# Attention with forget gates and an MLP on one core: the opening order rewritten, the first keys and queries in two token parts, w_in in column quarters

## The chip, the cores and the metric

The program runs on one core of a Trainium2 chip. The metric is device time in microseconds of one execution, the median over several. Three runs of the kernel before gave 329.88, 330.83 and 330.89 us, so the median is 330.83 us. One further execution was recorded by the hardware profiler; every row below is from that one.

## The reference

```python
def _attn_ref(q, k, v, f):            # each 8 batches, 8 heads, 576 tokens, 64 wide; f without the 64
    scores = scale * np.matmul(q, k.transpose(0, 1, 3, 2))
    cum = np.cumsum(np.log(np.clip(f, 0.0001, 1.0)), axis=-1)
    decay = cum[:, :, :, None] - cum[:, :, None, :]
    scores = np.where(causal, -1000000000.0, scores + decay)
    scores = scores - np.max(scores, axis=-1, keepdims=True)
    attn = np.exp(scores)
    attn = attn / (np.sum(attn, axis=-1, keepdims=True) + 1e-09)
    return np.matmul(attn, v)
...
x = attn_out.transpose(0, 2, 1, 3).reshape(4608, 512)
h = x @ w_in                          # 512 x 2048
g = 0.5 * h * (1.0 + np.tanh(c * (h + 0.044715 * h * h * h)))
return g @ w_out                      # 2048 x 512
```

All inputs and the output are float32; the kernel multiplies in bfloat16.

## The kernel before

**Tiling.** The 64 pairs of batch and head are worked in 16 *quads* of four heads (quad i is batch i // 2, heads 4 (i % 2) to 4 (i % 2) + 3). The 4608 tokens are worked through the MLP in nine *chunks* of 512. A chunk can start when the attention of its tokens is done, so chunk 0 needs the quads 0 and 1 (batch 0), chunk 1 the quads 2 and 3 as well, and so on.

**One quad.** Keys and queries (288 KB each as bfloat16) are loaded by POOL with a cast (`load_one`, L185), one load for all 576 tokens. VectorE turns each into its transposed form (`transpose_words`, L191). TensorE multiplies keys by queries (`scores`, L238) in rounds; ScalarE takes the exponential (L264); the diagonal blocks are masked by POOL (L270, word M) or by a VectorE product (L299, word m). TensorE forms denominators (word D) and the attention output (word V); VectorE scales the latter into `xT` (L355). The values are multiplied by the decay weights into `vw` (L210; word VW on POOL, vw on VectorE). The quads 0 and 1 are split by tokens into a part of 256 and a part of 320 (`parts`, L183; `split_rounds`, L60), so that the MLP of the first 256 tokens (*half tile*, `mlp_in_half`, L450) can start early.

**The MLP.** Chunk 0's first product runs in eight half-tile pieces (word J.half.g: 16 matmuls of 256 columns, then one Gelu of 128x1024 on ScalarE). Piece g needs the columns 512 g to 512 g + 511 of w_in. Its second product (`mlp_out`, L565) is a generator that is pulled in units of one 128-token tile by one block of 128 rows of w_out: the words F.0.n and f.0.n pull n units; f uses four matmuls of 32 columns for each of F's one of 128. There are 64 units, tile by tile, 16 blocks each. Chunk 1's first product is the word I (eight times, L369), its second is `seven_products` (L491), pulled by F.1.n and f.1.n. From chunk 2 on a table for each chunk (`TABLES`) says the order; these tables do the same work before and after the change.

**Order.** Nothing is scheduled by the machine: every engine runs its own instructions in the order in which the program emits them. `setup` (L584) emits the first loads, fills and the transposes of log f; then `FRONT` (L73), a string of words, says the order up to the start of chunk 2. `@` after a word makes its first DMA wait for a named earlier one. Words: LK, LQ load keys and queries, TK, TQ transpose them; WI loads a quarter of w_in (a column half of two of the four row blocks, L173), WO a quarter of w_out (four of its 16 row blocks); LP, LX load values on POOL's queue, LU, LV on SP's; S and H emit scores for four or for two heads; CW makes the decay weights; U sums blocks of w_out; X and Y load ScalarE's table for Exp and for Gelu; CL copies the low block of `vw`; B.n.c emits n matmuls of c columns on zeros, which only keep TensorE busy.

**Queues.** Loads that cast can only be issued by POOL. POOL issues them in its own instruction order, between masks and `vw`. At most eight POOL loads are in flight: the ninth waits for the first of them. All loads share 16 DMA engines.

**Pools.** `psS` has two buffers for scores and half-tile pieces, `psO` one for D and V, `psM` two for the split D and V and for the second product.

Of the kernel before, what the change touches and what calls it, by code (L numbers as in the profile page):

```python
# [8 lines left out]
FP32 = mybir.dt.float32  # L9
# [7 lines left out]
def kernel(  # L17
# [28 lines left out]
    CH = 512  # L46
# [22 lines left out]
    SETUP = """  # L69
        TK.0 LP.4 LP.0 LP.1  # L70
    """

    FRONT = """  # L73
        TQ.0 B.2.256 TK.1 SB TR LP.2@LQ.0 B.2.128 CW S.0.0 B.5.384 B.1.256 Z TQ.1 vw.0.0 S.0.2 WI.0 LQ.2 M.0.0 B.3.384 H.1.0.1
        LP.3 B.1.256 vw.1.0 WI.1@LU.4 W H.1.1.1 WI.3 B.2.256 WI.2 H.1.0.0 M.1.0.1 D.0.0 M.1.0.0 H.0.1.1 V.0.0.0 H.0.1.0 B.2.256 M.0.1 H.1.1.0 V.0.1.0
        D.1.0 H.0.3.0 B.2.128 V.1.0.0 LX.1.1 H.0.3.1 V.1.1.0 m.0.3.2 H.1.3.0 m.0.3.4 B.1.256 VW.1.1 H.1.3.1 B.4.128 vw.0.1 D.0.1 M.1.3 S.1.2 M.1.1 LK.2
        V.0.1.1 V.0.0.1 WO.0 J.0.1 D.1.1 J.0.0 WO.1@LV.1.1 V.1.1.1 V.1.0.1 J.0.3 WO.2@WI.1 VW.3 J.1.0 WO.3 LK.3 LQ.3 J.1.1 TQ.2 J.1.3 LQ.4
        LX.1.0@WO.2 TK.2 J.0.2 J.1.2 X LK.4 F.0.6 TK.3 B.3.256 S.2.0 LK.5 F.0.9 S.2.2 F.0.10 S.2.1 TQ.3 TQ.4 F.0.10 LV.2.0@LK.5 m.2.1 vw.2
        TK.4 S.3.0 f.0.1 M.2.2 CL.2 LQ.5 M.2.0 D.2 f.0.6 S.3.1 m.3.0 F.0.6 V.2.0 S.3.2 TK.5 LK.6 M.3.2 f.0.7 V.2.1 CL.3
        S.4.1 m.3.1 LQ.6 F.0.6 TQ.5 H.4.2.1 D.3 H.4.0.1 LQ.7 VW.4 H.4.0.0 V.3.1 v.3.0 f.0.3 H.4.2.0 CL.4 I.1.0 m.4.1 U.0 LV.2.1@LQ.5 I.1.4  # L80
        TQ.6 m.4.2.3 I.1.1 I.1.5 U.1 LV.3.0@LQ.7 m.4.2.2 TK.6 G.0 M.4.0 I.1.2 I.1.3 U.3 I.1.6 I.1.7 G.1.1.2 U.2 X F.1.14 S.5.0 f.1.28 S.5.1 D.4 M.5.0 f.1.16
        S.5.2 V.4.0 m.5.2.3 f.1.10 VW.5 V.4.1 CL.5 m.5.2.2 LQ.8 S.6.0 f.1.10 M.5.1 D.5 f.1.7 S.6.1 V.5.1 f.1.12 V.5.0 vw.6 S.6.2
        m.6.1 M.6.2.2 m.6.0 m.6.2.3 LK.7 LK.8 CL.6 LX.3.1@LK.6
# [4 lines left out]
    TABLES.update(dict.fromkeys((2, 5), """  # L88
        Y O.512 P.0 P.1 TK.q3 TQ.q3 LK.q5 LQ.q5 TK.q4 TQ.q4 LK.q6 LQ.q6 LV P.4 P.5 G.0 P.2 P.3 P.6 P.7 G.1.1.2 X F.10 S.q3.0
        D.q2 M.q3.0 f.22 S.q3.1 V.q2.0 M.q3.1 VW.q3 f.18 S.q3.2 V.q2.1 M.q3.2 CL.q3 f.16 S.q4.0 D.q3 M.q4.0 f.18 S.q4.1 V.q3.0  # L90
        M.q4.1 VW.q4 f.9 V.q3.1 f.7 S.q4.2 M.q4.2 CL.q4
    """))
    TABLES.update(dict.fromkeys((3,), """
        Y O.512 P.0 P.1 TK.q3 TQ.q3 LK.q5 LQ.q5 TK.q4 TQ.q4 LK.q6 LQ.q6 LV K.1.0 K.1.1 K.1.2 P.4 P.5 G.0 P.2 P.3 P.6 P.7 G.1.1.2
        X F.10 S.q3.0 D.q2 M.q3.0 f.22 S.q3.1 V.q2.0 M.q3.1 VW.q3 f.18 S.q3.2 V.q2.1 M.q3.2 CL.q3 f.16 S.q4.0 D.q3 M.q4.0 f.18
        S.q4.1 V.q3.0 M.q4.1 VW.q4 f.9 V.q3.1 f.7 S.q4.2 M.q4.2 CL.q4
    """))
    TABLES.update(dict.fromkeys((4,), """
        Y O.512 P.0 P.1 TK.q3 TQ.q3 LK.q5 LQ.q5 TK.q4 TQ.q4 LK.q6 LQ.q6 LV K.3.0 K.3.1 K.3.2 P.4 P.5 G.0 P.2 P.3 P.6 P.7 G.1.1.2
        X F.10 S.q3.0 D.q2 M.q3.0 f.22 S.q3.1 V.q2.0 M.q3.1 VW.q3 f.18 S.q3.2 V.q2.1 M.q3.2 CL.q3 f.16 S.q4.0 D.q3 M.q4.0 f.18  # L100
        S.q4.1 V.q3.0 M.q4.1 VW.q4 f.9 V.q3.1 f.7 S.q4.2 M.q4.2 CL.q4
    """))
    TABLES.update(dict.fromkeys((6,), """
        Y O.512 P.0 P.1 TK.q3 TQ.q3 LK.q5 LQ.q5 LV P.4 P.5 G.0 P.2 P.3 P.6 P.7 G.1.1.2 X F.10 S.q3.0 D.q2 M.q3.0 f.22 S.q3.1
        V.q2.0 M.q3.1 VW.q3 f.18 S.q3.2 V.q2.1 M.q3.2 CL.q3 f.16 D.q3 f.18 V.q3.0 v.q3.1 T K.1.3 K.3.3 f.18
    """))
    TABLES.update(dict.fromkeys((7,), """
        Y O.512 P.0.1 R.1 P.4.1 R.1 R.1 R.3 P.2.1 R.3 G.0.1.2 P.6 R.3 G.0.3.4 G.1.1.2 T
    """))
    TABLES.update(dict.fromkeys((8,), """  # L110
        O.512 P.0.1 R.1 P.4.1 R.1 R.1 R.3 P.2.1 R.3 G.0.1.2 P.6 R.3 G.0.3.4 G.1.1.2
    """))
# [60 lines left out]
    def load_w_in(c):  # L173
        n, u = D_FF // 2, c % 2
        s = slice(n * (c // 2), n * (c // 2 + 1))
        return nc.gpsimd.dma_start(out=w_in_sb[:, 2 * u:2 * u + 2, s], in_=w_in_hbm[:, u, :, s])
# [8 lines left out]
    def load_one(src, dst, i):  # L185
        b, h0 = i // QPB, 4 * (i % QPB)
        return nc.gpsimd.dma_start(
            out=dst[i % 2].rearrange("p a d -> p (a d)"),
            in_=src[b, h0:h0 + 4].rearrange("h (p a) d -> (h p) (a d)", p=32))

    def transpose_words(src, dst):  # L191

        nc.vector.transpose(  # L193
            out=dst.rearrange("p s c -> p (s c)").bitcast(FP32)
                .rearrange("p (t a) -> p a t", a=S // 32),
            in_=src.rearrange("p a d -> p (a d)").bitcast(FP32)
                .rearrange("p (a d) -> p a d", d=D // 2),
        )

    def transpose_k(i):  # L200
        transpose_words(k_c[i % 2], kT[i % 2][:, 64:64 + S])

    def transpose_q(i):
        transpose_words(q_c[i % 2], qT[i % 2])
# [245 lines left out]
    def mlp_in_half(half, g):  # L450

        ph = psS.tile([128, 2, 512], FP32, name="ps_h", tag="s")
        n0 = QA * half
        for dts in (range(N_DT - 1), range(N_DT - 1, N_DT)):
            for j in range(4):
                ft = 4 * g + j
                for dt in dts:
                    nc.tensor.matmul(  # L458
                        ph[:, j // 2, QA * (j % 2):QA * (j % 2) + QA],
                        w_in_sb[:, dt, 128 * ft:128 * ft + 128],  # L460
                        xT[:, dt, n0:n0 + QA],
                        start=(dt == 0 and j % 2 == 0), stop=(dt == N_DT - 1),
                        skip_group_check=True,
                    )
        nc.scalar.activation(gT[:, 4 * g:4 * g + 4, n0:n0 + QA],
                             ph.rearrange("p a (b n) -> p (a b) n", n=QA), AF.Gelu_apprx_tanh)
# [98 lines left out]
    def mlp_out(c):  # L565

        for n in range(CH // 128):
            r0 = CH * c + 128 * n
            st = ostage_pool.tile([128, D_MODEL], FP32, name="o_st", tag="o")
            pso = psM.tile([128, D_MODEL], FP32, name="pso", tag="m")  # L570
            for ft in range(N_FT):
                cols = 32 if by_columns else 128
                for c0 in range(0, 128, cols):
                    nc.tensor.matmul(pso[c0:c0 + cols, :],  # L574
                                     gT[:, ft, 128 * n + c0:128 * n + c0 + cols],
                                     w_out_sb[:, ft, :],
                                     start=(ft == 0), stop=(ft == N_FT - 1), skip_group_check=True)
                if ft == N_FT - 1:
                    nc.vector.tensor_copy(st, pso)
                    nc.sync.dma_start(out=out[r0:r0 + 128, :], in_=st)  # L580
                yield


    def setup():  # L584
# [195 lines left out]
```

## Time and profile before

| what | value |
|---|---|
| span of the profiled execution, first to last instruction | 328.4 us |
| median of the three timed runs | 330.83 us, 2.4 us above that span |
| TensorE busy | 316.9 us (96%) |
| ScalarE, VectorE, POOL busy | 201.7, 206.4, 110.6 us |
| moved by DMA | 33.42 MB, 16.58 MB of it on POOL's queue |
| chain that ended last, TensorE's share | 86% |
| first score matmuls of quad 0, start | 9.78 us |
| first exponential of quad 0, start | 10.64 us |
| first half-tile piece (J.0.1), start | 24.94 us |
| first scores of quad 3 (S.3.0), start | 51.17 us |
| start of chunk 1's first product, of chunk 2's | 66.93 us, 102.42 us |

The profile gives busy time by engine, the span cut into 40 slices, groups by source line, and the chain of work that ended last, followed back from the last instruction to what released each step. A stretch can be cut out and its busy time and DMA rate read alone. Matmuls are pipelined: a row's busy time is a little longer than what it adds to the chain.

### The profile page before, as it was taken

The page shows a single profiled execution, that of the slowest core. Times are in us where ns is not written, and L with a number is a line of the kernel's source. Part 1 is how long each engine was busy: PE and PEld are TensorE (multiplying, and loading weights), DVE is VectorE, ACT ScalarE, POOL GpSimd, SP SyncE. Part 2 cuts the span into 40 slices and gives each one's busy share as a digit, 9 for nine tenths or more (in the row PEclk, how much of TensorE's full clock was granted, in tenths as well). Part 3 has the DMA queues.
Part 4 walks back from the last instruction along what each step waited for, and adds up shares of the span by engine and source line. Part 5 has one row for each costly group of instructions (what it writes and reads, how often), then busy time and mean ns, then how long its engine had stood idle before and what let it go on. Part 6 is the DMA issues. An engine that isn't in the chain of part 4 may idle for free.

```text
span 328.4 us, 11961 instructions
## 1 busy us (share of the span) xinstructions
PE 316.9 (96%) x5421; PEld 206.5 (63%) x5421; DVE 206.4 (63%) x323; ACT 201.7 (61%) x231; POOL 110.6 (34%) x155
## 2 busy tenths in 40 slices
PE   3999999999999999999999999999999999999995
PEld 1458844545776477646774577557754777787684
DVE  4686039884887865674567456636553767875772
ACT  4685576866767586668656775768675841721630
POOL 8985572510504415520544054303440140000000
PEclk9999999999999999999999999999999999999999
DMA  7999999861124990295129711761110102002012
GB/s 123 210 214 215 168 230 199 167 165 24 36 40 94 236 208 31 94 187 108 37 68 182 140 37 36 160 122 36 36 66 0 36 21 81 2 32 98 0 35 96
DMA packets 44323, 33.42 MB, mean 102 GB/s; under 512 B 27488, under 2 KB 37856, under 8 KB 44272
## 3 DMA queue, kind: packets, MB, share of 16 engines
q0 software_dynamic: 8848, 16.58, 28.0%
q1 hardware_dynamic: 35280, 16.01, 18.4%
q8 instruction: 42, 0.69, 0.9%
q14 instruction: 9, 0.07, 0.1%
q10 hardware_dynamic: 144, 0.07, 0.1%
HBM read 36.85 MB, written 9.44 MB: 141 GB/s over the span
## 4 chain that ended last, share of the span: by engine, by line
PE 86%; DMA 3%; DVE 3%; ACT 3%; POOL 2%; issue 2%; POOLq 0%; DVEq 0%; ACTq 0%
PE ps_h L369 29%; PE ps_w L504 25%; PE po L324 9%; PE ps_s L256 8%; PE pso L574 4%; PE ps_h L458 4%; DMA v_nat<-in_v_dram 2%; PE ps_cd L417 2%; ACT pt L264 2%; PE ps_ab L417 2%; PE po_m L310 1%; POOL vw L210 1%; DMA out_dram<-o_st 1%; POOL v_nat L164 0%; PE ps_o L324 0%
## 5 line engine op out<-in xcount | busy, mean ns | idle before, releaser
L264 ACT ACTIVATE pt<-ps_s 128x1024 bf16<-128x1024 f32 (+2 forms) x100 | 93.7, 988 | 39.4 <-PE ps_s L256 34.9
L369 PE MATMUL ps_h<-xT,w_in_sb 128*128 128x512 bf16 x448 | 99.0, 379 | 0.0
L376 ACT ACTIVATE gT<-ps_h 128x1024 bf16<-128x1024 f32 x56 | 57.2, 1022 | 49.9 <-PE ps_h L369 48.3
L270 POOL TENSOR_SCALAR_AFFINE_SELECT pt<-pt 128x512 bf16<-128x512 bf16 (+3 forms) x65 | 38.2, 597 | 132.9 <-ACT pt L264 131.8
L369 PEld LDWEIGHTS <-w_in_sb 128*128 128x128 bf16 x448 | 43.8, 98 | 50.1 <-issue 0.4
L504 PEld LDWEIGHTS <-gT 128*32 128x32 bf16 (+1 forms) x1253 | 50.9, 97 | 6.4 <-issue 1.7
L504 PE MATMUL ps_w<-w_out_sb,gT 128*32 128x256 bf16 (+1 forms) x1056 | 46.9, 273 | 0.0
L504 PEld LDWEIGHTS <-gsum 128*32 128x32 bf16 (+1 forms) x1256 | 38.9, 97 | 2.7 <-issue 1.4
L256 PE MATMUL ps_s<-qT,kT 32*128 32x64 bf16 (+5 forms) x896 | 36.8, 263 | 0.3 <-ACT pt L264 0.2
L483 DVE TENSOR_TENSOR gsum<-gT 128x1024 bf16<-128x1024 bf16 x16 | 11.0, 689 | 35.2 <-ACT gT L376 35.2
L504 PE MATMUL ps_w<-usum,gsum 128*32 128x256 bf16 (+1 forms) x832 | 30.7, 273 | 1.0 <-ACT snap L525 0.7
L355 DVE TENSOR_TENSOR xT<-po,rb 128x576 bf16<-128x576 f32 x26 | 19.6, 755 | 18.9 <-PE po L324 18.6
L193 DVE STREAM_TRANSPOSE kT<-k_c 128x576 f32<-128x576 f32 x16 | 20.0, 1247 | 17.8 <-DMA k_c<-in_k_dram 17.8
L210 POOL TENSOR_TENSOR vw<-v_nat,wT 128x1280 bf16<-128x1280 f32 (+1 forms) x13 | 30.4, 2338 | 0.1
L529 DVE TENSOR_TENSOR o_st<-ps_w,snap 128x512 f32<-128x512 f32 x31 | 21.3, 689 | 13.2 <-PE ps_w L504 11.8
L256 PEld LDWEIGHTS <-kT 32*128 32x128 bf16 x896 | 16.9, 93 | 17.4 <-issue 12.6
L324 PE MATMUL po<-pt,vw 128*32 128x64 bf16 (+4 forms) x624 | 22.5, 279 | 0.0
L324 PEld LDWEIGHTS <-vw 128*32 128x32 bf16 x672 | 14.3, 96 | 10.6 <-issue 3.7
L193 DVE STREAM_TRANSPOSE qT<-q_c 128x576 f32<-128x576 f32 x16 | 19.9, 1242 | 1.1 <-PE ps_s L256 0.5
L164 POOL DMA_DIRECT2D v_nat<-in_v_dram x20 | 15.3, 776 | 4.6 <-DMA w_out_sb<-in_moe_w_out_dram 4.6
L504 PE MATMUL ps_w<-usum,gT 128*128 128x256 bf16 (+1 forms) x197 | 16.4, 273 | 0.0
L574 PE MATMUL pso<-w_out_sb,gT 128*32 128x512 bf16 (+1 forms) x115 | 15.6, 380 | 0.0
(97 smaller groups left out, 327.0 us busy)
## 6 DMA issues: line engine op xcount, KB each, us to landing
out_dram<-o_st SPq DMA_DIRECT2D x35, 256.0 KB, 2.4
k_c<-in_k_dram POOLq DMA_DIRECT2D x16, 288.0 KB, 5.8
q_c<-in_q_dram POOLq DMA_DIRECT2D x16, 288.0 KB, 7.3
v_nat<-in_v_dram SPq DMA_DIRECT2D x16, 256.0 KB, 8.5
w_in_sb<-in_moe_w_in_dram POOLq DMA_DIRECT2D x4, 512.0 KB, 9.5
w_out_sb<-in_moe_w_out_dram POOLq DMA_DIRECT2D x4, 512.0 KB, 8.3
v_nat<-in_v_dram SPq DMA_DIRECT2D x16, 128.0 KB, 3.5
v_nat<-in_v_dram POOLq DMA_DIRECT2D x13, 128.0 KB, 6.9
```

What stands on the lines that cost most here:

```text
L193: nc.vector.transpose(out=dst.rearrange("p s c -> p (s c)").bitcast(FP32) .rearrange("p (t a) -> p a t", a=S // 32), in_=src.rearrange("p ...
L210: eng.tensor_mul(vw[i % 2][:, t0:t1], vb[:, t0:t1, h0:h0 + 4, :], wT[:, i, t0:t1, :].unsqueeze(3).to_broadcast([128, t1 - t0, 4, D]))
L256: nc.tensor.matmul(tiles[h // 2][:, h % 2, c0:c0 + nq], key_columns(i, key, h, c), qq[32 * h:32 * h + 32, q0:q0 + nq, c], start=(c == 0 an ...
L264: nc.scalar.activation(p[:, 2 * g:2 * g + 2, off:off + n], t[:, :, 0:n], AF.Exp, scale=scale)
L270: nc.gpsimd.affine_select(out=x, in_=x, compare_op=ALU.is_ge, fill=0.0, base=0, pattern=pattern, channel_multiplier=-1)
L324: nc.tensor.matmul(po[r0:r0 + w.shape[-1], 448 + q0:448 + q0 + nq], w, p[:, h, col:col + nq], start=(key in (0, "low")), stop=(key in ("lo ...
L355: nc.vector.tensor_mul(xT[:, 2 * u + x, S * b + s0:S * b + s1], po, rbs[i, part])
L369: nc.tensor.matmul(ph[:, j, :], w_in_sb[:, dt, 128 * ft:128 * ft + 128], xT[:, dt, CH * c:CH * (c + 1)], start=(dt == 0), stop=(dt == N_DT ...
L376: nc.scalar.activation(gT[:, 2 * pr:2 * pr + 2, :], ph, AF.Gelu_apprx_tanh)
L504: nc.tensor.matmul(ps[c0:c0 + width, n, cols[0]:cols[1]], x[:, j, 128 * n + c0:128 * n + c0 + width], w[:, j, cols[0]:cols[1]], start=(fir ...
L529: nc.vector.tensor_add(st, ps, kept[name])
L574: nc.tensor.matmul(pso[c0:c0 + cols, :], gT[:, ft, 128 * n + c0:128 * n + c0 + cols], w_out_sb[:, ft, :], start=(ft == 0), stop=(ft == N_F ...
```

## The change

The setup is dissolved into words of FRONT, and FRONT is written anew up to chunk 2.

- The keys and queries of the quads 0 and 1 are loaded in two token parts each (LQ.0.0 is the first 256 tokens of quad 0's queries), eight loads in place of four, ahead of all of w_in, and each part is transposed by itself. The source of a part is indexed by head (4), then partition (32), then a contiguous run of 512 or 640 numbers; a whole load's source merges into 128 runs of 1152.
- w_in is loaded in eight pieces, column quarter c and row half u, in place of four.
- The values of batch 0 are loaded on SP's queue in place of POOL's.
- The zeros and the sums before each block move from POOL to VectorE; the fillers B are 17 matmuls of 256 columns, 15 of them at the very start.
- The first half-tile piece J.0.0 is put in two portions (word h) between the last scores of quad 1, in psO's buffer. Its Gelu and those of the other pieces are emitted one step later (word j).
- `mlp_out` walks two token tiles side by side, four row blocks of w_out at a time (first blocks 0 to 3 of both tiles, then 4 to 7, and so on).
- In chunk 1, the masks of the quads 4 to 6 go to POOL, and after chunk 1's first product come the denominators of quad 4 (word D.4) and only six units before the next scores (S.5.0), in place of S.5.0 after 14.

```diff
-    SETUP = """
-        TK.0 LP.4 LP.0 LP.1
-    """
     FRONT = """
+        LQ.0.0 FD ID MI B.15.256 LK.0.0 LQ.1.0 LF MS TQ.0.0 TK.0.0 PT LQ.0.1 LU.1 CP UT H.0.0.0 H.0.0.1 LK.1.0 TQ.0.1 TK.1.0 sb LU.0@LQ.1.0 TR TQ.1.0
+        C1 LK.0.1 C2 EW z H.0.2.1 LQ.1.1 H.1.0.0 W TK.0.1 B.2.256 WI.0.1 H.1.0.1 LK.1.1 TQ.1.1 M.0.0 vw.0.0 D.0.0 VW.1.0 m.1.0.0 WI.0.0 H.0.1.1 WI.2.0
+        V.0.0.0 H.0.1.0 V.0.1.0 H.0.3.0 M.1.0.1 D.1.0 H.0.3.1 M.0.1 TK.1.1 V.1.1.0 m.0.3.4 m.0.3.2 LU.2@LQ.1.1 WI.1.0 WI.1.1 WI.2.1 H.0.2.0 V.1.0.0
+        H.1.1.0 D.0.1 LQ.2 H.1.1.1 WI.3.1 LU.3 WI.3.0 H.1.2.0 h.0.0.1 LK.2 LU.4 VW.1.1 H.1.2.1 h.0.0.1 vw.0.1 S.1.3 V.0.1.1 M.1.1 j V.0.0.1 J.0.1 j
+        m.1.3.2 m.1.3.4 D.1.1 WO.0 J.0.2 WO.2 V.1.0.1 j LX.1.0 V.1.1.1 Y J.0.3 j J.1.0 TK.2 j J.1.1 j WO.1 TQ.2 J.1.2 j LQ.3 WO.3 U.0 LK.3 TQ.3 LX.1.1
+        VW.2 J.1.3 j CL.2 X F.0.7 S.2.0 f.0.10 LK.4 LQ.4 S.2.1 M.2.1 LV.2.0@LK.4 F.0.7 H.2.2.1 TK.3 H.2.2.0 f.0.7 M.2.0 S.3.0 M.2.2 f.0.3 D.2 f.0.1
...
+        TK.5 I.1.7 CL.4 I.1.6 I.1.1 G.1.1.2 I.1.5 X D.4 f.1.6 TK.6 CL.5 S.5.0 f.1.3 f.1.5 f.1.3 V.4.0 M.5.0 G.0 f.1.5 f.1.2 S.5.1 V.4.1 VW.6 f.1.5
...
-    def load_w_in(c):
-        n, u = D_FF // 2, c % 2
-        s = slice(n * (c // 2), n * (c // 2 + 1))
+    def load_w_in(c, u):
+        n = D_FF // 4
+        s = slice(n * c, n * (c + 1))
...
-    def load_one(src, dst, i):
+    def load_one(src, dst, i, part=None):
         b, h0 = i // QPB, 4 * (i % QPB)
+        if part is not None:
+            s0, s1 = parts[part]
+            return nc.gpsimd.dma_start(
+                out=dst[i % 2][:, s0 // 32:s1 // 32].rearrange("p a d -> p (a d)"),
+                in_=src[b, h0:h0 + 4, s0:s1].rearrange("h (p a) d -> h p (a d)", p=32))
...
+        for n0 in range(0, CH // 128, 2):
+            pso = [psM.tile([128, D_MODEL], FP32, name="pso", tag="m") for n in range(2)]
+            for (f0, m) in [(f0, m) for f0 in range(0, N_FT, 4) for m in range(2)]:
+                n = n0 + m
+                for ft in range(f0, f0 + 4):
```

## The prediction

> **What bounds the kernel now.** I read the page's slices first.
>
> ```profile
> PE   3999999999999999999999999999999999999995
> DMA  7999999861124990295129711761110102002012
> GB/s 123 210 214 215 168 230 199 167 165 24 36 40 94 236 208 31 94 187 108 37 68 182 140 37 36 160 122 36 36 66 0 36 21 81 2 32 98 0 35 96
> ```
>
> A slice is 8.2 us. TensorE is busy in all but the first; DMA is at its limit only in the first seven. So the time is TensorE's work plus what it loses, and it can lose much only in the opening, where all data still has to come. Everything from chunk 2 on (102.42 us in this trace) is the same program after the change, so I ask one thing: how much earlier does chunk 2's first product start?
>
> Next the chain of waits, cut to 10 to 55 us (start, duration, what):
>
> ```profile
> 16.88 2.65 ACT pt L264 x3
> 19.61 0.83 ACT pt L264
> 20.52 0.82 ACT pt L264
> 21.36 1.40 DVE pt L299
> ...
> 25.00 1.85 PE ps_h L458 x16
> ...
> 30.50 10.59 PE ps_h L458 x96
> 41.08 1.29 PE pso L574 x6
> 42.38 0.33 PE idle_ps L235 x3
> ...
> 51.24 0.63 PE ps_s L256 x20
> ```
>
> The reader is to see two regimes. To 22.8 us ScalarE's exponentials of the quads 0 and 1 end each step. From 23.6 us on it is TensorE alone: J.0.1 at 25.00, quad 3's first scores (S.3.0) at 51.24.
>
> Last, DMA in stretches (busy time of each engine in columns, then granted clock, DMA share, GB/s), the queue's wait, and a wait at chunk 1's product:
>
> ```profile
> 33.00:35.00 2.00, 2.00 (x21) 1.79 (x19) 0.64 (x1) 1.28 (x2) 2.00 (x1) 1.00 0.95 131
> 35.00:45.60 10.60, 10.60 (x104) 7.37 (x106) 0.02 (x1) 7.54 (x9) 5.98 (x10) 1.00 1.16 193
> ```
> ```profile
> DVE kT L193 <- DMA k_c<-in_k_dram: 14.6, 4, 11.9
> ```
> ```profile
> PE ps_w L504 <- ACT snap L525: 0.7, 1, 0.7
> ```
>
> The 11.9 us wait ends at 45.58, when quad 3's keys (K3) land. Its scores are needed only at 51.24, so before the change loads are on time by 4.4 us (51.24 less 45.58 and 1.26 for the transpose). That is the margin which an earlier TensorE uses up.
>
> **The change, part by part.**
>
> *First exponential.* Before, it waits for K0 whole (its transpose starts at 5.76), Q0 (7.50), then the weights' table and sums, and starts at 10.64. After, the first 256 tokens are enough. LQ.0.0 is issued at 1.32 like K0 before; LK.0.0 follows the identity on POOL, at about 2.5. K0 took 4.4 us from issue to its transpose with 288 KB; 128 KB at 165 GB/s (K0 to Q0: 288 KB in 1.74 us) are 0.8 us against 1.8, but the values' 256 KB (LU.1) now share the engines, so I take 3.8: landing at 6.3. Transpose 1.26 × 256/576 = 0.56, scores 0.4: 7.4 us, just when ScalarE's table for Exp is there (6.12 + 1.28). So 3.2 us earlier.
>
> *The exponentials.* ScalarE's work is the same: 0.67 for the decay weights and 12.6 for sixteen exponentials (1.51 + 9.81 + 1.30 in the trace). From 7.4 without a pause that ends at 20.7. But VectorE now has, ahead of the sums before each block, the transposes TQ.0.1 and TK.1.0, whose parts are fourth and fifth in POOL's queue (944 and 1072 KB with all ahead of them: 7.2 and 7.9 us by bytes, about 8.3 and 9.2 as K1 came late, too). TK.1.0 to 9.8, four small sums 0.6, the second product 1.2 (8.63 to 9.88 in the trace): the decay weights start at about 11.6, not 8.9, a pause of 2.7. The end is 23.4, against 24.95 before.
>
> *J.0.1.* It needs the second column quarter of w_in. Ahead of it and with it: 144 KB (f), 1152 (keys, queries), 1152 (values), five pieces of 256: 3728 KB = 3.82 MB, at the 188 GB/s of the next paragraph 20.3 us from 2.1; K1 (1.03 MB, 7.6 by count, 9.49 in fact) and the values landed up to 2 us behind such a count, so 22.4 to 24. I take 23.3, 1.7 before 25.00. By then J.0.0 is done between exponentials (1.85 less to do; its cover is TensorE's wait for ScalarE, and without the cover it costs its 1.75). The filler at 42.38 goes: 0.33. TensorE by itself would so be 1.7 + 1.75 + 0.33 = 3.8 us earlier.
>
> *Loads for quad 3.* Up to K3's landing the old order moved 144 + 1152 + 1152 + 2048 (w_in) + 576 (Q2, K2) + 576 (values) + 2048 (w_out) + 288 = 7984 KB = 8.18 MB in 45.58 − 2.1 = 43.5 us: 188 GB/s. The new order has Q3 ahead of K3, too: 8272 KB = 8.47 MB, 45.0 us, landing 47.1. It fills two holes: 33 to 35 (131 GB/s for 193: 0.6 us) and about 2.9 to 3.5, where little moves (0.4, by LU.1). I take 46.7. Transpose and semaphores 1.4: S.3.0 at 48.1. On the way the blocks 4 to 7 of w_out (WO.1, 7.36 MB ahead of and with it: 41.2 us by the same rate) hold unit 8: the eight pieces end at about 37.4 and seven units and S.2.0 at 39.5, so TensorE waits 1.7, then 9 units, S.2.1, 7 units, two half scores and 7 units (23 × 0.227 + 0.57 + 1.12 = 6.9) make 48.1 as well. **So TensorE comes early and the loads catch it.**
>
> Progress at S.3.0 is not equal: before, 35 units are done there, after, 31 (7 + 10 + 7 + 7; a unit is 2.27/10 = 0.227), but two half scores (0.56 each) in place of one whole (0.57). The old order's equal point is 51.24 − 0.91 + 0.55 = 50.9. Gain 50.9 − 48.1 = **2.8 us**.
>
> *From S.3.0 to chunk 2.* The same products, the same scores, as many half scores in all. Before, nothing but the 0.7 row above stops TensorE: the copy of the first sum waits behind the Exp table (1.28 + 0.20) and two exponentials. The new order has D.4 (0.8), 17 units and V.4.0 ahead of unit 32, so the copy is done: **0.7 us** gained. Masks that go from VectorE (0.42) to POOL (0.62) cost nothing while POOL, 34% busy, is ahead of D.5; uncovered, 0.2 each. Zeros and sums on VectorE: counted in the pause above. The out stores stand behind LV.2.0 on SP, which waits for K4; three staging buffers cover it. The paired walk of `mlp_out` has the same matmuls: nothing. Bounds of this stretch, as no row shows its new waits: 1 us gained (all of TensorE's idle and latency near 81 to 86) to 2 us lost (three waits of one copy each, 0.7).
>
> *Split loads.* No row shows a load whose source begins with 4 heads. The nearest, whole keys and half w_in, move at 179 to 209 GB/s in the stretches 3.4 to 9.5 and 14.2 to 25. I take that rate. Bounds: 216 GB/s (25 to 33 us, values among them) and the slower rival's.
>
> Sum: 2.8 + 0.7 = 3.5 us off a span of 328.4 gives 324.9; 2.4 lie around it to the median of 330.8, so 327.3. I take **327.4**.
>
> **Rivals.**
>
> *Loads keep up* (they come faster, or K3 is not last). At 216 GB/s K3 would land at 41.3 and no load stops TensorE; it is then 3.8 us ahead by J.0.1, and up to 5.3 if the weights come at 21.8, when a buffer is free, and the 0.7: 324.8 to 326.3, about 325.6. For it: 193 GB/s at 35 to 45.6, more than the average I used, and 250 at 46 to 50. Against: those with high rates carry values, and the order ahead of K3 is w_out's cast.
>
> *Split loads on few engines: slower.* If a load is dealt to engines by the outermost extent of its source, a part uses 4 of 16. With the four always the same, these carry all 1.18 MB of first keys and queries plus a sixteenth each of the rest: 0.295 + 0.456 = 0.75 MB each at 188/16 = 11.75 GB/s, 63.9 us; K3 lands at 66, S.3.0 at 67.4, 16.5 late, 0.7 back: 346.6. If the four change from load to load, the fullest engine has 0.082 in place of 0.074 MB: 0.7 us, and the forecast stands nearly. It turns slower than before when the fullest engine has 41 KB, 8%, more than the mean (K3 at 50.2, S.3.0 at 51.6). A modest imbalance, 0.1 MB, gives 8.5 us on K3's landing and some 335.8. For it: whole loads have an outermost extent of 128, and K1 and the values landed behind their byte count, which only uneven engines explain. Against: nothing in the trace shows a load on few engines.
>
> The Trainium skill, "DMA: Bandwidth & Descriptors", section "Why a DMA increments its semaphore by 16 and not by 1", says that a DMA runs on the largest number of engines up to 16 that divides both slowest extents, here 4, and that on POOL's path the group moves on from load to load. By that rule the first keys land later but the sum moves by the 0.7 us above only; no row of this trace can show it.
>
> *Nothing gained.* The change moves the wait: chunk 1's new order loses in two or three places (0.7 each, like the copy) and the loads come 1 us later than taken; 330 to 331.5. For: POOL issues w_in and w_out between masks and `vw` that wait for ScalarE, in order. Against: eight loads in flight are some 11 us of data, longer than any such wait.
>
> **Chances.** Forecast (326.3 to 329.7): 0.50. Loads keep up: 0.22. Nothing gained (within 0.3%, 1 us, about what a measurement of this kernel can tell from no change): 0.13. Slower by split loads: 0.15. Faster by over 0.3%: 0.72; same 0.12; slower 0.16. The range leaves out the far end of the slower case: 324.6 to 331.2.
>
> **What would show it.** First exponential near 7.4; J.0.1 near 23.3; TensorE waiting at unit 8 for w_out and at S.3.0 for K3's transpose, S.3.0 at 48; no wait for the copy (L549 after the change); chunk 2 at 99. If TensorE waits for no load from 24 to 50, the first rival; if the first transposes start after 9 us and K3 lands after 50, the second; if S.3.0 is at 48 and chunk 2 at 102, the third. I would be wrong above all if 188 GB/s is not the rate of the new mix.

## The result and the profile after

The changed kernel takes 340.00 us (median of four runs, 339.58 to 340.47) against 330.69 us for the kernel before (four runs, 329.88 to 330.89). The ratio is 1.0286, 95% interval 1.0266 to 1.0306: slower by 9.3 us, where 3.5 us less were forecast. The profiled execution has a span of 338.8 us (before: 328.4). Some of the kernels below show two levels of time from run to run; where it matters, the single times are given.

The slices of the page after (TensorE, its granted clock, DMA share and GB/s, 8.5 us each) answer to those shown of before:

```profile
PE   4499999989979999999999999999999999999995
PEclk9556999999999999999999999999999999999999
DMA  6999999879103887049104920390120012002012
GB/s 81 154 146 164 194 224 193 179 155 186 30 2 72 202 164 144 30 123 206 54 7 133 202 65 13 102 205 2 37 95 0 4 35 96 2 31 95 0 33 94
```

Two things are new, both at the front. The first slices move 81 and 154 GB/s where before moved 123 and 210. And TensorE's clock stands at half, or little over it, in the second to fourth slice, of which two read 9 in TensorE's busy row: a full digit at half clock hides a loss. New gaps in that row stand only in the slices 2, 9 and 12.

The chain of waits in the opening (start, duration, what):

```profile
3.99 9.59 DMA q_c<-in_q_dram
...
13.61 0.74 DVE qT L198
...
20.01 1.21 DVE vw L217
...
21.27 0.51 PE po_m L317 x7
21.78 0.97 PE ps_s L263 x8
...
34.78 1.85 PE ps_h L467 x16
```

Before, ScalarE's exponentials ended each step here, and J.0.1 started at 25.00. Now the second part of quad 0's queries ends the waiting: its load takes 9.59 us, VectorE turns it at 13.61 and works off what stands behind it to 21.2. From 21.27 TensorE alone is the chain, but eight score products take 0.97 us, where the chain of before had

```profile
16.28 0.58 PE ps_s L256 x8
```

J.0.1 starts at 34.78, 9.8 us late. The same stretch by windows (busy time of TensorE, its weight loads, VectorE, ScalarE, POOL, then granted clock, DMA share, GB/s):

```profile
18.00:22.00 4.00, 3.16 (x37) 1.40 (x38) 3.84 (x11) 2.82 (x4) 2.38 (x3) 0.50 0.77 149
22.00:26.00 4.00, 4.00 (x52) 1.44 (x48) 3.25 (x8) 2.60 (x3) 2.91 (x6) 0.50 0.99 130
29.00:33.00 4.00, 4.00 (x32) 2.10 (x24) 2.38 (x4) 2.32 (x3) 3.74 (x5) 0.61 1.15 183
33.00:36.00 3.00, 3.00 (x70) 2.30 (x69) 1.52 (x4) 2.32 (x3) 2.70 (x4) 1.00 1.13 151
```

From 22 us TensorE is busy 4.00 of 4.00 us at 0.50 of its clock, and it comes back to 1.00 only at about 32 us. Later the chain reads:

```profile
58.42 0.64 PE ps_s L263 x22
...
64.49 1.93 ACT pt L271 x2
...
66.48 2.58 POOL pt L277 x3
...
75.39 0.35 PE ps_h L376
...
95.93 2.75 DVE gsum L509
...
112.67 0.21 PE ps_h L376
```

and the waits of TensorE from 40 to 125 us (total, times, longest):

```profile
PE ps_w L528 <- DVE gsum L509: 2.3, 1, 2.3
PE po L331 <- POOL pt L277: 0.8, 1, 0.8
PE pso L598 <- issue: 0.2, 1, 0.2
```

S.3.0 starts at 58.42, 7.5 us behind the equal point of before (50.9 in the prediction). No load stops TensorE there. The wait for the copied sum (0.7 before) is gone, but one of 2.3 us for VectorE's `gsum` and one of 0.8 for POOL's masks are new. Chunk 1's first product starts at 75.39 (67.00 before), chunk 2's at 112.67 (102.42): 10.25 late, and with the chunks that follow in step (the profiled execution ends 10.4 later) that is the whole loss there. So the account to be settled is: 9.8 late at J.0.1, of which 2.3 come back by S.3.0, where J.0.0 and a filler are no longer to be done (1.75 + 0.33 in the prediction); 7.5 there; 2.4 more by the three waits (2.3 + 0.8 − 0.7); and 0.35 in smaller pieces.

### The profile page after: what moved, and what is told of

Read it like the earlier page. It is cut to its first block, busy times and chain, and to the rows that moved or that the text cites. A ratio compares the mean times of both kernels' runs of the same rounds, so it can differ in the third digit from the quotient of the medians.

```text
span 338.8 us, 12230 instructions
## 1 busy us (share of the span) xinstructions
PE 319.3 (94%) x5542; PEld 207.5 (61%) x5560; DVE 202.0 (60%) x325; ACT 202.0 (60%) x233; POOL 119.1 (35%) x157
## 4 chain that ended last, share of the span: by engine, by line
PE 84%; DVE 6%; DMA 3%; POOL 3%; issue 2%; ACT 1%; POOLq 0%; DVEq 0%
PE ps_h L376 28%; PE ps_w L528 24%; PE ps_s L263 9%; PE po L331 8%; PE ps_h L467 5%; PE pso L598 3%; DMA q_c<-in_q_dram 3%; PE ps_cd L424 2%; PE po_m L317 2%; PE ps_ab L424 2%; POOL pt L277 1%; DVE gsum L509 1%; ACT pt L271 1%; POOL vw L217 1%; DVE kT L198 1%
## 5 line engine op out<-in xcount | busy, mean ns | idle before, releaser
L376 PE MATMUL ps_h<-xT,w_in_sb 128*128 128x512 bf16 x432 | 98.0, 379 | 0.8
L277 POOL TENSOR_SCALAR_AFFINE_SELECT pt<-pt 128x512 bf16<-128x512 bf16 (+2 forms) x75 | 46.4, 628 | 128.3 <-ACT pt L271 127.3
L263 PE MATMUL ps_s<-qT,kT 32*128 32x64 bf16 (+5 forms) x896 | 39.1, 274 | 5.2 <-DVE kT L198 4.6
L217 POOL TENSOR_TENSOR vw<-v_nat,wT 128x1280 bf16<-128x1280 f32 (+2 forms) x16 | 35.4, 2212 | 6.2 <-DMA v_nat<-in_v_dram 5.7
L263 PEld LDWEIGHTS <-kT 32*128 32x128 bf16 x896 | 17.7, 95 | 23.7 <-issue 13.7
L553 DVE TENSOR_TENSOR o_st<-ps_w,snap 128x512 f32<-128x512 f32 x31 | 21.2, 686 | 12.5 <-PE ps_w L528 12.4
L198 DVE STREAM_TRANSPOSE kT<-k_c 128x576 f32<-128x576 f32 (+2 forms) x18 | 20.1, 1116 | 11.7 <-DMA k_c<-in_k_dram 11.7
L198 DVE STREAM_TRANSPOSE qT<-q_c 128x576 f32<-128x576 f32 (+2 forms) x18 | 20.1, 1115 | 6.1 <-DMA q_c<-in_q_dram 6.0
L331 PE MATMUL po<-pt,vw 128*32 128x64 bf16 (+4 forms) x648 | 23.4, 278 | 0.0
L350 DVE STREAM_TRANSPOSE den<-po 128x576 f32<-128x576 f32 x14 | 10.9, 782 | 11.6 <-PE po L331 11.1
L528 PE MATMUL ps_w<-usum,gT 128*32 128x256 bf16 (+1 forms) x206 | 16.4, 273 | 0.0
```

What stands on the lines that cost most here:

```text
L198: nc.vector.transpose(out=dst.rearrange("p s c -> p (s c)").bitcast(FP32) .rearrange("p (t a) -> p a t", t=32), in_=src.rearrange("p a d - ...
L217: eng.tensor_mul(vw[i % 2][:, t0:t1], vb[:, t0:t1, h0:h0 + 4, :], wT[:, i, t0:t1, :].unsqueeze(3).to_broadcast([128, t1 - t0, 4, D]))
L263: nc.tensor.matmul(tiles[h // 2][:, h % 2, c0:c0 + nq], key_columns(i, key, h, c), qq[32 * h:32 * h + 32, q0:q0 + nq, c], start=(c == 0 an ...
L277: nc.gpsimd.affine_select(out=x, in_=x, compare_op=ALU.is_ge, fill=0.0, base=0, pattern=pattern, channel_multiplier=-1)
L331: nc.tensor.matmul(po[r0:r0 + w.shape[-1], 448 + q0:448 + q0 + nq], w, p[:, h, col:col + nq], start=(key in (0, "low")), stop=(key in ("lo ...
L376: nc.tensor.matmul(ph[:, j, :], w_in_sb[:, dt, 128 * ft:128 * ft + 128], xT[:, dt, CH * c:CH * (c + 1)], start=(dt == 0), stop=(dt == N_DT ...
```

## Experiments

Before the first record of the clock in a trace its column shows 1.00, so in the opening the clock is read from durations: eight score products of 320 columns take 0.6 us at full clock and 1.0 at half. The first experiments take parts of the change back out of the changed kernel. The second group adds parts to the kernel before.

### Undoing parts of the changed kernel

**e1_whole**: the keys and queries of the quads 0 and 1 loaded and transposed whole.

```diff
-        LQ.0.0 FD ID MI B.15.256 LK.0.0 LQ.1.0 LF MS TQ.0.0 TK.0.0 PT LQ.0.1 LU.1 CP UT H.0.0.0 H.0.0.1 LK.1.0 TQ.0.1 TK.1.0 sb
+        LQ.0 FD ID MI B.15.256 LK.0 LQ.1 LF MS TQ.0 TK.0 PT LU.1 CP UT H.0.0.0 H.0.0.1 LK.1 TK.1 sb
```

> The changed kernel, but the keys and queries of the quads 0 and 1 in four whole loads and whole transposes, in the same places of the order. Theory A (a split load runs on a quarter of the engines, so the fourth part lands at 13.6 us and everything after it is late): the decay weights start at about 13 us in place of 16.9, the exponentials of quad 1 end near 25 to 28 in place of 35.2, chunk 2 starts 6 to 9 us earlier: 331 to 334 us. Theory B (half clock of TensorE from 8.2 to 32.1 us paces the exponentials): the gap in TensorE's work stays, so the loss mostly stays, 336 us or more. Theory C (values on SP's queue take the engines from the first loads): no change, 339 to 341.

339.02 us, ratio to before 1.0237 (1.0195 to 1.0279). J.0.1 comes at 32.98, 1.8 earlier. From 15.6 on TensorE is the chain, but at half clock (eight scores 0.97), and it takes to 33 us. Of the 1.8 us only 0.15 are left at chunk 2 (112.52 for 112.67): in this execution the clock falls to half for 3.4 us behind the 2.3 us wait for `gsum`. So split loads are not the only cause: behind them stands a second one.

**e2_warm**: 28 fillers after the transposes of log f and 22 after the first sums.

```diff
-        TK.0.0 PT LQ.0.1
+        TK.0.0 PT B.28.256 LQ.0.1
...
-        C1 LK.0.1 C2 EW
+        C1 LK.0.1 B.22.256 C2 EW
```

> The changed kernel with 28 more idle matmuls of 256 columns ahead of the first scores and 22 ahead of the second product of the decay weights, so that TensorE has no long gap. Theory B: the clock stays full, the exponentials after the decay weights follow each other without a pause (about 11 us from 17 in place of 17.6 to 35.2), J.0.1 starts at 29 to 31 in place of 34.7: 334 to 337 us. Theory A alone: first exponential at 11.1 and decay weights at 16.9 as before, and the time within 1 us of 340.

340.40 us, ratio 1.0281. The clock is full from 4.4 to 18.1 us, falls there and stays at half to about 31.7; J.0.1 at 34.43. A clock warmed ahead of the work is lost again within it.

**e3_values**: the values' first load (LU.1) gated behind LK.0.0.

```diff
-        LQ.0.1 LU.1 CP
+        LQ.0.1 LU.1@LK.0.0 CP
```

> The changed kernel with the first load of values (LU.1, on SP's queue) waiting for the first keys' first part. Theory C: LQ.0.0 lands at about 4.5 and the fourth part 3 us earlier than 13.6; 337 us or less. Theory A: LQ.0.0 lands no earlier than 6.5, the fourth part within 1.5 us of 13.6, the time within 1.5 us of 340.

340.42 us, ratio 1.0271. The fourth part is turned 1.8 us earlier (11.82 for 13.61), but `vw` then waits for the values until 19.2, and J.0.1 comes at 34.26. Bytes of values do slow the parts; moving them only moves the wait.

**e4_g0**: chunk 1's first products in the order 0, 4, 1, 5, with the sums G.0 right behind.

```diff
-        VW.5 I.1.2 TQ.5 LQ.7 I.1.0 I.1.4 I.1.3
-        TK.5 I.1.7 CL.4 I.1.6 I.1.1 G.1.1.2 I.1.5 X
+        VW.5 I.1.0 TQ.5 LQ.7 I.1.4 I.1.1 I.1.5
+        G.0 TK.5 I.1.2 CL.4 I.1.3 I.1.6 I.1.7 G.1.1.2 X
```

> The changed kernel with the pieces of chunk 1's first product in the old order (0, 4, 1, 5, then the Gelu sums of the first half, then 2, 3, 6, 7), so that these sums are done long before unit 32. Theory D (the wait of 2.3 us for these sums in chunk 1 is a loss of its own): 337.5 to 338.5 us. If TensorE would otherwise wait for another thing there: within 1 us of 340.

338.07 us, ratio 1.0215 (1.0179 to 1.0250): 1.9 us off. The 2.3 us wait for `gsum` is gone, 1.1 for VectorE's `xT` is new: 1.2 net. In the profiled execution J.0.1 came 1.3 us earlier as well, for which the edit gives no reason, so the 1.9 is not all the wait's.

**e5_fill**: e2_warm and two to four fillers behind each group of scores.

```diff
-        V.0.0.0 H.0.1.0 V.0.1.0 H.0.3.0 M.1.0.1 D.1.0 H.0.3.1 M.0.1
+        V.0.0.0 B.2.256 H.0.1.0 B.2.256 V.0.1.0 H.0.3.0 B.2.256 M.1.0.1 D.1.0 H.0.3.1 B.2.256 M.0.1
```

> The changed kernel with idle matmuls of 256 columns in TensorE's gaps up to the decay weights (28 and 22) and two to four behind each score group of the exponentials' stretch. Theory B (half clock paces the stretch from 20 to 33 us, which in the last four runs was TensorE's work alone with 1.0 us for eight score matmuls): full clock from about 5 us on, eight matmuls in 0.6 us, J.0.1 at 29 to 31 in place of 34.7, 334 to 337 us. If the decay weights' lateness (16.9) alone sets the stretch: 339 to 341.

340.46 us, ratio 1.0298. The clock is full from 4.1 us through the opening (eight scores 0.55), J.0.1 at 32.12 and S.3.0 at 55.77, 2.7 earlier in spite of 2.3 us of fillers in the chain. Nothing of it is left at the end: behind the 2.3 us wait for `gsum` the clock falls to half (TensorE's mean from 80 to 100 us is 0.91), and in chunk 2 TensorE idles 1.1 us for no reason that the profile names. Chunk 2 starts 1.1 earlier and chunk 3 0.1 later than in the changed kernel.

**e6_sums**: the sums before each block ahead of the second parts' transposes on VectorE.

```diff
-        LQ.0.1 LU.1 CP UT H.0.0.0 H.0.0.1 LK.1.0 TQ.0.1 TK.1.0 sb
+        LQ.0.1 LU.1 CP UT sb H.0.0.0 H.0.0.1 LK.1.0 TQ.0.1 TK.1.0
```

> The changed kernel with the sums ahead of each block (word sb) emitted before the transposes TQ.0.1 and TK.1.0, so that VectorE does them at about 10.2 us and not at 14.9. Theory E (VectorE's order behind the late fourth part holds the decay weights): decay weights at 13 to 14 us in place of 16.9, and 1 to 4 us off the time: 336 to 339. Theory B alone: the half clock still paces everything behind, 339 to 340.5.

339.63 us, ratio 1.0281. The decay weights come 3.4 us earlier (13.54), J.0.1 only 1.6 (33.19): `vw` now waits for the values, which land at 18.86, and from 19.7 on TensorE at half clock is the chain.

**e7_three** (e4_g0, e6_sums and the fillers of e5_fill, with 4 for 22 ahead of C2) and **e8_whole3** (e7_three with the first loads whole).

> The changed kernel with the idle matmuls, the early sums and the old order of chunk 1's first product together; loads in parts as changed. Theory B with E and D: J.0.1 at 25 to 28, 329 to 333 us. If the split loads alone are the cause (theory A): 335 or more.

> The same three, and the keys and queries in whole loads. Theory A adds to the others: 1 to 3 us below the kernel with parts, 328 to 331. If parts cost nothing once the clock is full: within 1 us of the kernel with parts.

e7_three: 344.34, 338.78, 345.56, 338.44 us; e8_whole3: 335.17, 336.36, 344.31, 343.78. The profiled execution of e7_three is the one of 344.34: the clock falls at 16.9 us, and a pair of fillers then takes 0.54 us of the chain, not 0.33 (J.0.1 at 39.17). That of e8_whole3 (335.17, span 333.5) has the full clock throughout: J.0.1 at 28.77, S.3.0 at 52.43. So the same fillers help where the clock holds and cost more where it falls. And even at its best, with whole loads and full clock, the new order is 1.5 us behind before's equal point, with TensorE, fillers among its work, the chain from 7.9 to 58 us, and 5 us at the end.

### Adding parts to the kernel before

**e9_order**: all edits of the change to the code, with w_in in quarters, but the words of FRONT in the old order (WI.0 becomes WI.0.0 WI.1.0, J.0.1 becomes J.0.1 j, and so on).

> All edits of the change to the code, with w_in in quarters and the second product in pairs of row tiles, but the order of the work as before (first loads whole, all fillers, old chunk 1). Theory: the loss is in the new order of the opening and of chunk 1, so this stands within 1 us of before, 330 to 332 us, chunk 2 at 102 to 103.5 us. Rival: the quarters of w_in (shorter packets) or the paired second product cost some of it: 333 us or more, with TensorE waiting for w_in or w_out between 25 and 60 us.

335.36 us, ratio 1.0159 (1.0143 to 1.0176). I had expected no loss; the rival had named the quarters, but with a wait for w_in or w_out. J.0.1 comes at 29.1. The only new wait of TensorE in the opening, and the windows around it (columns as above):

```profile
PE po_m L316 <- POOL pt L276: 1.1, 1, 1.1
```
```profile
18.00:20.00 2.00, 1.63 (x26) 0.82 (x23) 0.88 (x3) 2.00 (x3) 1.99 (x4) 1.00 1.13 255
20.00:22.00 2.00, 1.27 (x27) 0.58 (x27) 0.92 (x4) 0.88 (x2) 2.00 (x4) 0.96 1.24 206
22.00:24.00 2.00, 2.00 (x29) 0.84 (x25) 1.38 (x4) 1.25 (x2) 1.93 (x4) 0.50 1.24 203
24.00:26.00 2.00, 2.00 (x23) 0.97 (x25) 1.26 (x3) 1.62 (x2) 1.46 (x3) 0.50 1.24 205
26.00:28.00 2.00, 2.00 (x40) 0.85 (x32) 1.12 (x3) 0.55 (x1) 2.00 (x4) 0.50 1.17 282
```

TensorE idles 1.1 us for a mask (19.6 to 20.7), and at 21.8 us its clock falls to half for 6.8 us, although it is busy all of that time.

**e13_halves**: e9_order with w_in in the four pieces of before.

```diff
-        n = D_FF // 4
+        n = D_FF // 2
...
-        WI.0.0 WI.1.0 LQ.2
+        WI.0.0 LQ.2
```

> e9_order with w_in loaded in the four pieces of before (column halves), all else as in e9_order. Theory Q, the four more issues of the quarters stand ahead of a mask on GpSimd, TensorE idles 1.1 us at 19.6 us, and the clock falls to half for 7 us: with halves the wait goes, the first MLP product starts at 25.0 to 25.6 us (29.1 in e9_order), 330.0 to 331.5 us. Rival, the paired second product or other code of the change costs it: 334 to 336 us still.

330.56 us (twelve runs), ratio 1.0003 (0.9985 to 1.0021), J.0.1 at 24.84. This is the kernel before, with the paired second product and all the other code of the change at no cost. Its windows:

```profile
18.00:20.00 2.00, 2.00 (x48) 1.08 (x46) 1.17 (x4) 2.00 (x3) 1.28 (x3) 1.00 1.07 253
20.00:22.00 2.00, 1.98 (x37) 1.05 (x31) 1.80 (x4) 1.92 (x4) 2.00 (x4) 1.00 1.12 208
22.00:24.00 2.00, 1.82 (x50) 0.94 (x49) 2.00 (x4) 1.13 (x2) 2.00 (x3) 1.00 1.11 207
```

So the quarters alone, in the old order, cost 4.8 us. They are four more issues of 0.7 us each in POOL's queue ahead of masks that TensorE needs: six of them end at 19.4 in e9_order, three at 16.8 in e13_halves, and the masks start there. The clock makes 4.3 us at J.0.1 out of a wait of 1.1.

**e11_nofill**: the kernel before without its fillers up to the first MLP product (they compute nothing that is used).

> The kernel before, with all filler products up to the first MLP product left out (they compute nothing that is used). Theory B, the fillers hold TensorE's clock up in the exponentials' stretch: without them eight score products take 1.0 us and not 0.58 from about 8 us to 25 us or longer, the first MLP product starts at 27 to 31 us in place of 25.0, and the time is 332 to 336 us. Rival, TensorE has enough idle time there that the slower clock is hidden: first MLP product at 24.5 to 25.5 us, 330 to 331 us.

334.96 us, ratio 1.0134 (1.0119 to 1.0150); J.0.1 at 28.25, 3.25 late. From the chain:

```profile
16.14 0.44 PE po_m L310 x8
16.58 0.97 PE ps_s L256 x8
17.54 0.44 PE po_m L310 x4
...
26.10 2.15 PE po_m L310 x20
28.25 1.82 PE ps_h L458 x13
```

Eight scores take 0.97 where before's chain had 0.58 at 16.28: half clock, and TensorE, not ScalarE, is the chain from 16 us on. The fillers are no idle padding: with them before's opening is bound by exponentials, without them by a slow TensorE.

**e10_split** (e9_order) and **e15_splithalf** (e13_halves), both with the first keys and queries in two parts, one behind the other:

```diff
-        FD LK.0 LQ.0 ID LK.1 LQ.1 UT
+        FD LK.0.0 LK.0.1 LQ.0.0 LQ.0.1 ID LK.1.0 LK.1.1 LQ.1.0 LQ.1.1 UT
```

> The kernel with the old order (e9_order), the first keys and queries of quads 0 and 1 loaded and transposed in two token parts each, both parts of a tensor one behind the other, nothing else moved. Theory A, parts of four heads go over a quarter of the DMA engines and land late: the last part lands 2 us or more behind the whole load's landing, the first exponentials come 1 to 3 us later, and the time is 331.5 to 334 us. Rival, parts are as fast as their bytes: within 0.5 us of e9_order.

> e10_split with w_in in the four pieces of before: the two token parts alone against e13_halves. Theory A, four more issues and parts that land late, and eight loads in flight that the ninth must wait for: first exponentials 3 to 4 us later than e13_halves, sums on GpSimd late by as much, time 3 to 6 us above e13_halves. Rival, e10_split's loss was again that of the clock after the quarters: within 1.5 us of e13_halves.

e10_split: 341.21 us, ratio 1.0320 (1.0295 to 1.0345), 5.85 above e9_order. e15_splithalf: 338.32 us, ratio 1.0263 (1.0200 to 1.0327), in single runs 336.25, 336.42, 340.22 and 341.22. In its profiled execution (336.25) the clock holds, and the whole loss can be read. DMA in e13_halves (whole loads) and then in e15_splithalf (parts), last column GB/s:

```profile
3.00:5.00 2.00, 0.07 (x1) 0.11 (x2) 0.45 (x1) 0.68 (x1) 1.93 (x6) 1.00 0.96 156
5.00:7.00 2.00, 2.00 (x11) 1.39 (x11) 1.26 (x1) 1.25 (x3) 2.00 (x3) 1.00 1.08 159
7.00:9.00 2.00, 0.99 (x3) 0.29 (x2) 1.26 (x1) 0.50 (x1) 1.76 (x6) 1.00 1.05 184
```
```profile
3.00:5.00 2.00, 0.08 (x1) 0.11 (x2) 0.45 (x1) 0.68 (x1) 1.93 (x5) 1.00 0.62 31
5.00:7.00 2.00, 1.44 (x9) 0.88 (x9) 0.00 (x0) 1.26 (x3) 2.00 (x4) 1.00 0.92 71
7.00:9.00 2.00, 0.96 (x2) 0.50 (x2) 0.64 (x1) 0.49 (x1) 1.59 (x4) 1.00 0.77 105
```

and the chain of e15_splithalf:

```profile
1.34 0.89 POOL k_c L189
2.23 7.50 DMA k_c<-in_k_dram
9.72 0.28 issue
10.01 0.94 POOL v_nat L164
...
11.06 8.78 DMA v_nat<-in_v_dram
19.84 0.03 issue
```

The parts start at 31 and 71 GB/s where whole loads have 156 and 159. A part of 160 KB takes 7.50 us, and since only eight POOL loads are in flight, POOL's next values wait for it. They land at 19.84, not 14.06 (e13_halves); J.0.1 starts at 30.71 (5.9 late) and chunk 2 at 108.56 (5.85 late, against e13_halves).

**e12_mid** (on e9_order), **e14_midhalf** and **e16_mid2** (on e13_halves): J.0.0 in two portions amid the last exponentials, its Gelu behind them, fillers there left out. In e12_mid and e14_midhalf D.0.1 stands ahead of the half tile, in e16_mid2 behind it as in the old order; this is the edit of e16_mid2. In all three the filler before S.2.0 goes as well.

```diff
-        m.0.3.4 B.1.256 VW.1.1 H.1.3.1 B.4.128 vw.0.1 D.0.1 M.1.3
+        m.0.3.4 h.0.0.1 VW.1.1 H.1.3.1 h.0.0.1 vw.0.1 D.0.1 M.1.3
...
-        WO.0 J.0.1 j D.1.1 J.0.0 j
+        WO.0 J.0.1 j D.1.1
```

> The kernel with the old order (e9_order), the first MLP half tile (J.0.0) computed in two parts amid the last exponentials in place of fillers there, its Gelu behind them, and one filler of 0.3 us at 42 us left out: the part of the change whose gain I still hold for real. If TensorE's idle time there takes it: 1.85 us gained against e9_order, 328 to 329.5 us, product J.0.3 1.85 us earlier. Rival, the loads (third quad's keys, w_out) end the wait instead: within 0.5 us of e9_order. Rival, the half tile holds up the scores: 0.5 to 2 us slower than e9_order.

> e12_mid with w_in in the four pieces of before: the first MLP half tile amid the last exponentials, in an opening that is else as before. If TensorE's idle time there takes it and the clock holds: 1.85 us off e13_halves, 328 to 329.5 us, below before. Rival, loads or vector copies end the wait before the second product: within 0.5 us of e13_halves. Rival, the clock falls after a gap as in e9_order: 333 us or more.

> e14_midhalf with the denominators of quad 0's second part back behind the half tile, as in the old order, so that the half tile covers VectorE's mask product that TensorE waited 1.27 us for in e14_midhalf. If that wait and the fall of the clock behind it were e14_midhalf's loss: no wait of over 0.4 us before 25 us, the clock holds, and of the 1.85 us what does not merely replace fillers (0.68) and idle time is gained: 329 to 330.3 us. Rival, the half tile itself holds the scores and exponentials up: 331.5 us or more at full clock.

e12_mid: 336.80 us, ratio 1.0192 (1.0158 to 1.0226), 1.4 above e9_order. e14_midhalf: 334.36, ratio 1.0144 (1.0091 to 1.0198); it waits 1.3 us for VectorE's mask product ahead of D.0.1 (21.5 to 22.8), and the clock falls at the end of that wait. e16_mid2: 335.92, ratio 1.0165 (1.0125 to 1.0206), runs 333.63 to 338.08. Its wait, and its windows:

```profile
PE ps_h L466 <- DMA w_in_sb<-in_moe_w_in_dram: 1.9, 1, 1.9
```
```profile
20.00:22.00 2.00, 1.27 (x26) 0.47 (x18) 1.81 (x4) 1.80 (x3) 2.00 (x4) 1.00 1.11 203
22.00:24.00 2.00, 0.85 (x5) 0.61 (x6) 1.62 (x3) 0.00 (x0) 2.00 (x3) 0.52 1.12 211
24.00:26.00 2.00, 2.00 (x15) 0.98 (x14) 0.00 (x0) 0.59 (x1) 0.94 (x1) 0.50 1.12 205
```

The expectation of a gain fell twice: the half tile needs w_in's second row half, which TensorE waits for until 23.15, too late to go amid the exponentials of this opening. Scores queue behind it, ScalarE has nothing to do (0.00 from 22 to 24), and the clock falls at 22.1, amid the wait. Runs whose mean clock was 0.999 or 1.000 still took 333.6 to 333.8, 3 us more than e13_halves; none of them was profiled, so what these 3 us are is not shown.

**e17_snap**: e13_halves with two units of chunk 1's second product ahead of S.5.0, and **e18_both**, this and e16_mid2.

```diff
-        F.1.14 S.5.0 f.1.28
+        F.1.14 f.1.2 S.5.0 f.1.26
```

> e13_halves with two units of chunk 1's second product moved ahead of the next scores, so that ScalarE copies the partial sum before the two exponentials and not behind them (TensorE waited 0.67 us for that copy). If nothing else is late there: 0.7 us off, 329.6 to 330.1 us. Rival, the exponentials or VectorE's sums (gsum) end the wait next: within 0.3 us of e13_halves.

> e16_mid2 and e17_snap together: if both hold, the sum of the two, 328.3 to 329.8 us, below both kernels. If the half tile costs the clock: as e16_mid2, less 0.7 us.

e17_snap: 330.50 us (twelve runs), ratio 1.0011 (0.9997 to 1.0026). The 0.67 us wait is gone and chunk 1, from its first product to chunk 2's, takes 34.96 us, not 35.42; chunk 2 gives 0.25 of that back, and the total does not move. e18_both: 335.92, ratio 1.0169 (1.0130 to 1.0208), as e16_mid2. No version tried beats the kernel before.

## Why the prediction was wrong

The direction was wrong, and two steps under it failed: the landing of the split loads, which I took at the rate of whole ones, and the fillers, which I costed at nothing. I named the fillers in the change but gave them no price, and took "TensorE's wait for ScalarE" as free room.

- *First exponential at 7.4, decay weights at 11.6.* Measured 11.11 and 16.93. The 128 KB of the first part were to take 0.8 us in DMA; quad 0's queries were turned at 7.89, its keys at 9.55, the second part of the queries at 13.61, where I had 8.3. (288 KB in 1.74 us is 169 GB/s, not the 165 that I wrote; it changes nothing.) With whole loads in the same places, e1_whole turns queries and keys at 6.99 and 8.70, still behind the 5.76 and 7.50 of before, and has its first exponential at 10.87 and the decay weights at 15.59. So halving the bytes made the first loads later, not earlier, and the new order would not have come near 7.4 without the split either. e15_splithalf shows the price of the split in the old order: 5.9 us at J.0.1, all of it kept to chunk 2.
- *Split loads.* I took the rate from whole loads, 179 to 216 GB/s; from 3 to 9 us of e15_splithalf it was 31 to 105. My slower rival had the right place but the wrong price: it counted how full the fullest engine gets in the long run (0.7 us when the four change), and not how long each part takes that the start waits for. In the trace of the changed kernel the data packets of POOL's queue in flight go up in steps of about four as loads are issued (about 4 at 4.2 to 4.6 us, 8 at 5.0 to 6.0, 12 at 6.4); with whole loads (e13_halves) there are 17 from 3.4 us on. The Trainium skill, "DMA: Bandwidth & Descriptors", section "Why a DMA increments its semaphore by 16 and not by 1", gives four engines, moving on, for such a load; the trace agrees. What I made of the rule, "the sum moves by the 0.7 us above only", was the error. The engines are not all of it: by 18 us of e15_splithalf the data packets of the parts (512 of 1024 bytes, 512 of 1280) take 142 us of engine time together and 3243 packets of 4 bytes another 29, where 612 packets of 2304 bytes of whole loads take 138 in e13_halves, with only 148 packets of 4 bytes beside them. No run separates the two.
- *The clock.* Not in the prediction. The changed order has 15 of its 17 fillers at the very start. Without fillers among the scores the clock stays at half from 8 to 32 us, and e11_nofill shows what that does alone: 3.25 us at J.0.1, 4.4 in the end. That this and the 5.9 of the split come near the 9.8 us by which J.0.1 is late is no account of it: in e15_splithalf the parts hold back values on POOL's queue, and the changed kernel has its first values on SP's. In the changed kernel the two causes overlap: undoing one leaves the other as the bound, so e1_whole and e5_fill gain 1.8 and 2.7 us there, and e8_whole3, which undoes both and does the sums early (e6_sums alone: 1.6), 6.0. The other 3.8 us belong to the new order; at S.3.0, where J.0.0 and a filler are behind it, 1.5 of them are left.
- *J.0.1 at 23.3, by the landing of w_in.* It came at 34.78; no load of w_in was awaited. The count of bytes was idle, since the start had been lost already. w_in's quarters were counted at nothing beyond their bytes; in the old order they cost 4.8 us (e9_order against e13_halves), as issues on POOL. What they cost in the changed kernel was not tried.
- *J.0.0 between the exponentials saves 1.75, the filler 0.33.* As work that need not be done later, this is what J.0.1's 9.8 gave back by S.3.0 (2.3). But the cover did not exist: e14_midhalf and e16_mid2 show that the gap it was to fill holds either fillers, which keep the clock, or nothing because w_in is not there yet. In the old order it is a loss of 3 us and more.
- *TensorE comes early and the loads catch it.* Never came to pass: S.3.0 at 58.42, not 48.1, with K3 turned at 54.16. The rival "loads keep up" failed with it: no load was awaited, and there was no gain.
- *0.7 us gained at the copy.* The wait went, as said; 2.3 us for `gsum` took its place (e4_g0 removed it, and 1.1 came back elsewhere). My bound for this stretch, 2 us lost, was passed: 3.1 lost, 0.7 gained. And e17_snap shows that taking the 0.7 away moves the total by less than can be measured.
- *Masks on POOL cost nothing.* D.3 waited 0.8 us for masks of quad 3, two of which (M.3.0 and M.3.1) also went from VectorE to POOL, though the list of the change names the quads 4 to 6 only. I had looked only at POOL's share of busy time. This wait was not undone in a run.

What stays open: e8_whole3 is still 5.1 us behind before in its span. Of that 1.5 us are there at S.3.0, 1.4 come by chunk 2 (1.2 of it in waits: 1.1 for `xT` and 0.8 for the masks, less the 0.7 at the copy), 1.35 are a wait of TensorE in chunk 2 that the profile calls "issue", and the remaining 0.85 was not traced. A wait of this last kind, of 1.1 to 2.5 us at 125 to 132 us, also stands in the profiled executions of e5_fill, e11_nofill, e12_mid, e14_midhalf, e16_mid2 and e18_both. In four of them (e11_nofill, e14_midhalf, e16_mid2, e18_both) the clock falls to 0.50 behind it, and chunk 2 takes 38.4 to 38.8 us, not 34.7. The traces have a candidate: loads of 16 KB on the instruction queue. In just these seven of the 20 traces two such loads that follow each other are 19.4 to 21.2 us apart; everywhere else they are at most 18.7 apart. The late one starts at most about 1.2 us before the gap, or at its start (e14_midhalf: load at 125.29, gap from 125.25). Whose instructions it brings the trace does not say. That TensorE waits for its program there fits, and was not tried. It would explain a good part of the spread of times, and not the loss of the changed kernel, whose chunk 2 took 35.0.

## What to carry to other kernels

Before you fill a gap in TensorE or take fillers out, ask what holds the clock there, and price the stretch at half clock as well: an engine that the profile shows as busy can be a slow one. When a first load is cut smaller, count the engines and in-flight slots that each piece gets and the issues it adds ahead of other work in that queue, not only its bytes. Put each part of a large reordering into the old kernel alone; parts taken out of the new one hide behind each other.

## What the runs showed of the hardware that was not expected

- A gap of 1.1 us in TensorE at 20 us (e9_order) amid small products is followed by 6.8 us at half clock, with TensorE busy 2.00 of 2.00 us from 22 to 28; in e16_mid2 the clock fell 0.8 us into a gap of 1.9. In the changed kernel it stayed at half from 22 to 28.7 us with no gap. The Trainium skill, "TensorE: Matmul & The Clock Gate", section "What's actually happening", has the clock go down after an idle window of about 3.4 us and up after one busy window of that length. The length agrees: the times between changes of the clock are multiples of 3.41 us in these traces. But less than half such a gap brought it down, and two windows in a row that read as fully busy did not bring it up; the measurement decides.
- What sorts the windows is work, not time. e11_nofill and the kernel before have the same scores and products on 32 rows or columns, without and with fillers on the whole 128 by 128 array: half clock without, full with. To test this over all 20 traces, cut each into the 3.41 us windows given by its clock records, and count a matmul as its columns times the share of the array that it uses. Of the windows without float32 products, all 1787 that kept the full clock have 3023 or more, and all 14 that lost it 2973 or less. The 17 that brought it up from half have 2800 or more, and 21 of the 22 that did not 2644 or less (one has 3034). Busy time does not sort them: windows that kept the clock were busy from 45%, and some that stayed at half 100%. Rows alone or columns alone do not either. This is a count over traces in which the ends of matmuls are modelled, and no kernel was built to test it.
- The same sum on VectorE (`gsum`, 128x1024) took 0.69 us in e4_g0 and 2.81 in the changed kernel, where POOL's `vw` of 2.4 us ran beside it. This is the 2.3 us wait above; that the two hold each other up was not tried apart.
